# Half of an expert goes from the attention part into the seven-product part

## The chip, the cores and the metric

One core of a Trainium2 chip runs the whole program. The metric is the device time of one execution in microseconds (us). A core has five engines, each with its own instruction queue that is worked off in order: TensorE (PE in the profile; its weight loads are shown as PEld), VectorE (DVE), ScalarE (ACT), GpSimd (POOL) and SyncE (SP). They meet through semaphores. Transfers are issued by SP, ACT or POOL and carried by 16 DMA engines. Matrix products go to PSUM; VectorE and ScalarE copy ("evict") them to SBUF.

## The reference

```python
def _attn_ref(q_l, k_l, v_l, q_g, k_g, v_g):          # 8 batches, 8 heads, 512 local and 32 global tokens, head size 64
    k_all = np.concatenate([k_g, k_l], axis=2); v_all = np.concatenate([v_g, v_l], axis=2)
    out_g = np.matmul(sm(scale * np.matmul(q_g, k_all.transpose(0, 1, 3, 2))), v_all)
    s_ll = np.where(np.abs(pos[:, None] - pos[None, :]) <= 32, scale * np.matmul(q_l, k_l.transpose(0, 1, 3, 2)), -1e9)
    s_lg = scale * np.matmul(q_l, k_g.transpose(0, 1, 3, 2))
    out_l = np.matmul(sm(np.concatenate([s_lg, s_ll], axis=-1)), np.concatenate([v_g, v_l], axis=2))
    return np.concatenate([out_g, out_l], axis=2)

def _moe_ref(x, w_gate, w1, w2):                      # x: 4352 tokens of 512; 8 experts, 512 -> 1024 -> 512
    P = np.exp(logits - logits.max())                 # logits = x @ w_gate
    for _ in range(8):                                # rows and columns brought to equal sums, eight times
        P /= P.sum(1, keepdims=True) + 1e-09
        P /= P.sum(0, keepdims=True) + 1e-09
        P *= N / E
    for e in range(E):
        out += P[:, e:e + 1] * (np.maximum(x @ w1[e], 0.0) @ w2[e])
```

Every expert works on every token, so the eight experts' products are most of the work. N is 4608 in the source; the 4352 rows of this case are what the kernel computes.

## The kernel before, in words

**First part: attention in slots.** A loop over `s` from 0 to 33 treats one pair of heads of one batch in each slot (32 pairs, four slots to a batch, and two slots to drain). Its stages lie staggered: while slot `s` computes the scores of pair `s`, pair `s-1` gets its output and pair `s+1` is transposed.
- `st_A` transposes keys and queries on TensorE (L305). VectorE copies the keys from PSUM into the row `kTe` (L307), ScalarE the queries into `qbd` (L314, two copies).
- `st_B` computes scores in three groups of 3, 3 and 2 blocks of 64 queries. A block takes two products: 128 columns of local keys (L337) and 32 of global keys (L339). VectorE adds the mask and takes the maximum (L344), ScalarE the exponential (L347). The first group of slot `s` needs `qbd` of the copies at the end of slot `s-1`.
- `st_D1` transposes the weights (L354; VectorE copies them, L356), `st_D2` transposes the finished output of pair `s-2` and the weights of the global keys (L364, L368; ScalarE copies both, L370 and L372), `st_E` multiplies with the values (L388; VectorE divides, L392 and L393).
- The global queries' attention is in `st_G1` (even slots; ScalarE L412, VectorE L409) and `st_G2`, `st_G3`, `st_G3n` (odd slots; ScalarE L422 and L449).

Between these stages lie places for **pieces** of experts 0 and 1, which are computed plainly on the 512 tokens of a group `m` as soon as the group's attention is done: `p_l1` (four products of 512 columns, L475, evicted by ScalarE at L478 or VectorE at L480) and `p_l2` (eight products, L489, evicted at L492, stored to DRAM as `yd`). A slot has six places: four `p_l1` (evicted by ACT, ACT, DVE, DVE) and two `p_l2` (both ACT). In units of four products of 512 columns that is 8 units a slot. The order of all queues is the order in which Python emits the instructions; no scheduler changes it.

GpSimd issues the loads that convert to 16 bits. In slots 8 to 32 it also forms, for experts 2 to 7, sums and differences of weight quarters (`sums_load`, `sums_form`, 24 steps of four `tensor_tensor`, L120) and stores them to DRAM as `kept`. SP moves the values into their second layout (`load_v`, `move`) and loads the global values `vgz` and `vgn`.

**Between the parts**, eight rounds of row and column sums (`sk_rows`, `sk_cols`) run on VectorE with small products on TensorE; the remaining pieces (`tail`) fill TensorE.

**Second part: seven products for eight.** Experts 2 to 7 run in 12 stages, two passes of six: pass 0 on the first 2048 tokens, pass 1 on the other 2304. Both matrix products of an expert are split into two by two quarters and computed with seven quarter products and sums of quarters. A stage has 8 slots in pass 0 and 9 in pass 1; a slot is a `Slot` (first product, L908) interleaved with a `Unit` (second product, L810), each product group at a fixed place in `run_slot`. ScalarE copies partial results, VectorE forms token sums (L749), sums of hidden activations (L806), rectified sums (L912), and adds results into the output (L844). `fetch` loads a stage's weights (L726) and their sums from `kept` (L727, L728). `stored_add` (L765) adds the stored results of experts 0 and 1 during the stages. In the first four slots of the first stage the pieces still left in `tail` fill TensorE (`fill`).

Of the kernel before, what the change touches and what calls it, by code (L numbers as in the profile page):

```python
# [23 lines left out]
def kernel(  # L24
# [33 lines left out]
    VW = Dh + 1  # L58
    assert (B, H, Sl, Dh, Sg) == (8, 8, 512, 64, 32) and D == H * Dh and F % P == 0
# [33 lines left out]
    work = {}  # L93

# [33 lines left out]
    with ExitStack() as att:  # L128
# [8 lines left out]
        mask = att_c.tile([P, 3, SW], FP32)  # L137
# [3 lines left out]
        kTe = [att_c.tile([P, W + Sl + W], FP16, name=f"kTe{i}") for i in range(4)]  # L141
        vgr = [att_c.tile([P, 4 * H * VW], FP16, name=f"vgz{i}") for i in range(2)]
        vgz = [t.rearrange("p (a h v) -> p a h v", a=4, h=H) for t in vgr]
        vgn = [att_c.tile([P, H, VW], FP16, name=f"vgn{i}") for i in range(2)]
# [4 lines left out]
        vg16 = [dscr.tile([Sg, H, Dh], FP16, name=f"vg16_{b}") for b in range(B)]  # L149

# [8 lines left out]
        def load_vz(b):  # L159
            for i in range(4):  # L160
                nc.sync.dma_start(out=vgz[b % 2][i:P:4, i, :, 0:Dh], in_=vg16[b])
            nc.sync.dma_start(out=vgn[b % 2][P - Sg : P, :, 0:Dh], in_=vg16[b])

        def load_v(b):
# [11 lines left out]
            def last():  # L176
                nc.gpsimd.dma_start(out=vb[HB : HB + W, NJ - 1, :, 0:Dh], in_=src[Sl - W : Sl])
# [10 lines left out]
            def move():  # L188
                if b < 2:
                    return part  # L190
                nc.sync.dma_start(out=vb[96:P, NJ - 1], in_=va[W : 2 * W, 0])
                nc.sync.dma_start(out=vb[0:HB, :], in_=va[HB:P, :])
                nc.sync.dma_start(out=vb[HB:P, 0 : NJ - 1], in_=va[0:HB, 1:NJ])
                if b > 1:
                    load_vz(b)
# [66 lines left out]
        for t in (kTe[0], kTe[2], kTe[3]):  # L262
            nc.vector.memset(t[:, 0:W], 0.0)
            nc.vector.memset(t[:, W + Sl :], 0.0)
# [7 lines left out]
        def clear_z(i, eng):  # L272
            eng.memset(vgr[i].bitcast(mybir.dt.uint32), 0)
            eng.tensor_copy(out=vgz[i][:, :, :, Dh], in_=own.unsqueeze(2).to_broadcast([P, 4, H]))
            eng.memset(vgn[i][0 : P - Sg], 0.0)
            eng.memset(vgn[i][P - Sg : P, :, Dh:VW], 1.0)
# [15 lines left out]
        load_vz(0)  # L292

# [3 lines left out]
        def st_A(n):  # L297
# [4 lines left out]
            for t, src in enumerate((ks, qs)):  # L302
                for so in range(NJ):
                    for a in range(2):
                        nc.tensor.transpose(pt[t][HB * a : HB * (a + 1), P * so : P * (so + 1)],  # L305
                                            src[:, 2 * hp + a, so, :], identity)
            nc.vector.tensor_copy(out=kt[:, W : W + Sl].rearrange("c (p s) -> c p s", s=NJ),  # L307
                                  in_=pt[0].rearrange("c (s p) -> c p s", s=NJ))
            if n < NPL:
                nc.scalar.copy(out=qpl[n % 2].rearrange("c (p s) -> c p s", s=NJ), in_=pt[1].rearrange("c (s p) -> c p s", s=NJ))  # L310
                return
            for a in range(2):
# [4 lines left out]
        def st_B(n, part):  # L317
# [10 lines left out]
            for ii in range(ni):  # L328
                i = i0 + ii
                if n < NPL:  # L330
                    for c0, c1, kk in ((0, KW, kt[:, HB * i : HB * i + KW]), (KW, SW, kgT[:, hp, Sg * b : Sg * (b + 1)])):
                        for a in range(2):
# [3 lines left out]
                    continue  # L336
                nc.tensor.matmul(sc[:, SW * ii : SW * ii + KW], qb[:, i, :],  # L337
                                 kt[:, HB * i : HB * i + KW], start=True, stop=True)
                nc.tensor.matmul(sc[:, SW * ii + KW : SW * (ii + 1)], qb[:, i, :],  # L339
                                 kgT[:, hp, Sg * b : Sg * (b + 1)], start=True, stop=True)  # L340
            for ii in range(ni):
                i = i0 + ii
                mi = 0 if i == 0 else (2 if i == NHB - 1 else 1)
# [54 lines left out]
        def st_G1(b, g):  # L398
# [3 lines left out]
            for c0, c1, k0 in ((0, Sl - W, 2 * W), (Sl - W, Sl, W), (Sl, S, None)):  # L402
                for hh in range(4):
                    pr, a = divmod(hh, 2)
                    r = slice(HB * a, HB * (a + 1))
                    rhs = kgT[r, 2 * g + pr, gc] if k0 is None else kTe[(n0 + pr) % 4][r, k0 : k0 + c1 - c0]
# [18 lines left out]
        def st_G3(b, g):  # L425
# [3 lines left out]
            for t in range(5):  # L429
                for par in range(2):  # L430
                    r, h0 = slice(HB * par, HB * (par + 1)), 4 * g + 2 * par
                    rhs = vb[:, t, h0 : h0 + 2, :] if t < NJ else vgn[b % 2][:, h0 : h0 + 2, :]
# [75 lines left out]
        NU = B * HP  # L508
        nc.vector.tensor_copy(out=mask[:, 0, 0:KW], in_=mask[:, 1, 0:KW])
        nc.vector.tensor_copy(out=mask[:, 2, 0:KW], in_=mask[:, 1, 0:KW])  # L510
        nc.vector.memset(mask[:, 0, 0:W], NEG)
        nc.vector.memset(mask[:, 2, 3 * W : KW], NEG)
        st_A(0)
        unread(2, 256)
        first_keys()
        for s in range(NU + 2):
            b, hp = divmod(s, HP)
            if s < NU and b + 1 < B:
# [15 lines left out]
                if s == 5:  # L534
                    queue += [lambda: load_g(1, "kgs"), lambda: load_g(1, "qgs")]
# [554 lines left out]
```

## Time and profile before

| what | value |
|---|---|
| time, median of 3 runs (range) | 998.58 us (998.53 to 999.15) |
| the profiled execution's own time | 998.93 us |
| its span, first to last instruction | 997.2 us |
| granted TensorE clock, mean | 0.998 |
| TensorE busy | 982.5 us (99%), 8868 products |
| VectorE busy | 767.2 us (77%) |
| ScalarE busy | 655.5 us (66%) |
| GpSimd busy | 301.7 us (30%) |
| first product of the second part (L908) | at 356.26 us |

The span is what the prediction's sums are made against; 1.7 us of the execution's own time lie outside it, and the own time is 0.35 us above the median. A row of a timeline gives start, duration, engine, line, operation, output and inputs, count, and in brackets how long the engine had waited and for whom. A row of a table of stretches gives the stretch, its length, and then for each engine the busy time and the number of instructions, the granted clock, and the DMA share. Durations of products overlap their successors, so the cost of a product is read from start to start.

### The profile page before, as it was taken

The page shows a single profiled execution, that of the slowest core. Times are in us where ns is not written, and L with a number is a line of the kernel's source. Part 1 is how long each engine was busy: PE and PEld are TensorE (multiplying, and loading weights), DVE is VectorE, ACT ScalarE, POOL GpSimd, SP SyncE. Part 2 cuts the span into 40 slices and gives each one's busy share as a digit, 9 for nine tenths or more (in the row PEclk, how much of TensorE's full clock was granted, in tenths as well). Part 3 has the DMA queues.
Part 4 walks back from the last instruction along what each step waited for, and adds up shares of the span by engine and source line. Part 5 has one row for each costly group of instructions (what it writes and reads, how often), then busy time and mean ns, then how long its engine had stood idle before and what let it go on. Part 6 is the DMA issues. An engine that isn't in the chain of part 4 may idle for free.

```text
span 997.2 us, 22451 instructions
## 1 busy us (share of the span) xinstructions
PE 982.5 (99%) x8868; PEld 641.0 (64%) x8868; DVE 767.2 (77%) x1858; ACT 655.5 (66%) x1342; POOL 301.7 (30%) x364
## 2 busy tenths in 40 slices
PE   7899999999999999999999999999999999999998
PEld 4566566656665555666666666676767676776764
DVE  7866665666653755889999888997899999888885
ACT  6888888888884566765555555557765555555551
POOL 9748887888850102111111111111111111100000
PEclk9999999999999999999999999999999999999999
DMA  9999999999952387554543333575664543123043
GB/s 167 186 156 199 239 206 221 222 200 222 234 144 85 108 241 169 161 147 121 122 107 74 75 75 74 128 214 129 165 148 117 117 96 66 53 65 74 2 106 127
DMA packets 138058, 138.68 MB, mean 139 GB/s; under 512 B 56608, under 2 KB 110048, under 8 KB 135904
## 3 DMA queue, kind: packets, MB, share of 16 engines
q0 software_dynamic: 105696, 87.32, 49.6%
q1 hardware_dynamic: 31696, 49.60, 15.5%
q8 instruction: 69, 1.13, 0.5%
q10 hardware_dynamic: 560, 0.33, 0.1%
q14 instruction: 37, 0.30, 0.1%
HBM read 144.46 MB, written 39.58 MB: 185 GB/s over the span
## 4 chain that ended last, share of the span: by engine, by line
PE 94%; POOL 3%; DMA 1%; DVE 1%; issue 0%; SPq 0%; ACT 0%; POOLq 0%; DVEq 0%
PE z L810 30%; PE pa L908 18%; PE py L489 12%; PE ph L475 12%; PE pb L908 9%; PE pc L908 4%; PE po L388 1%; PE ptw L354 1%; PE zp L879 1%; PE sc L337 1%; DMA vgz<-vg 1%; PE pk L305 1%; PE tgx L364 1%; PE pq L305 1%; PE sg L407 0%; POOL va L174 0%
## 5 line engine op out<-in xcount | busy, mean ns | idle before, releaser
L810 PEld LDWEIGHTS <-hs 128*128 128x128 f16 x2264 | 220.7, 98 | 91.8 <-DVE hs L806 0.4
L810 PE MATMUL z<-w2e,hs 128*128 128x256 f16 x1304 | 195.6, 273 | 0.0
L810 PE MATMUL z<-v,hs 128*128 128x256 f16 x960 | 144.0, 273 | 0.0
L475 PE MATMUL ph<-xT,w1e 128*128 128x512 f16 (+1 forms) x576 | 129.3, 367 | 0.6 <-ACT xT L372 0.6
L347 ACT ACTIVATE Pu<-ms,mx 128x160 f16<-128x160 f32 x256 | 120.1, 636 | 13.3 <-DVE mx L344 10.4
L489 PE MATMUL py<-w2e,hT 128*128 128x512 f16 x544 | 128.2, 379 | 0.0
L831 ACT COPY z<-z 128x256 f32<-128x256 f32 x98 | 35.0, 357 | 141.7 <-PE z L810 141.7
L908 PEld LDWEIGHTS <-w1e 128*128 128x128 f16 x960 | 87.1, 98 | 51.6 <-issue 1.0
L908 PE MATMUL pa<-t,s 128*128 128x512 f16 x384 | 114.2, 379 | 0.0
L726 POOL DMA_DIRECT2D w1e<-in_moe_w_dram x24 | 17.5, 734 | 297.5 <-PE pa L908 220.4
L344 DVE CUSTOM_DVE_ANT_0 ms<-sc,mask 128x160 f32<-128x160 f32 x256 | 70.2, 320 | 46.6 <-ACT yst L492 30.0
L844 DVE SCALAR_TENSOR_TENSOR oy<-z,lg,oy 128x512 f32<-128x512 f32 x128 | 95.8, 749 | 7.6 <-ACT oy L849 5.1
L806 DVE TENSOR_TENSOR hs<-hs 128x512 f16<-128x512 f16 x224 | 94.9, 424 | 8.2
L912 DVE CUSTOM_DVE_ANT_0 hx<-pb,s 128x512 f16<-128x512 f32 x96 | 65.9, 687 | 36.4 <-ACT s L942 30.2
L726 POOL DMA_DIRECT2D w2e<-in_moe_w_dram x24 | 19.8, 833 | 243.6 <-PE z L810 214.2
L928 ACT ACTIVATE hs<-pa 128x512 f16<-128x512 f32 x96 | 57.2, 596 | 47.0 <-PE pa L908 46.9
L475 PEld LDWEIGHTS <-w1e 128*128 128x128 f16 x576 | 53.4, 98 | 52.9
L912 DVE CUSTOM_DVE_ANT_0 hs<-pb,s 128x512 f16<-128x512 f32 x96 | 65.9, 686 | 24.1 <-ACT s L942 23.7
L908 PEld LDWEIGHTS <-s 128*128 128x128 f16 x720 | 65.6, 98 | 28.5 <-issue 0.3
L489 PEld LDWEIGHTS <-hT 128*128 128x128 f16 x544 | 49.8, 98 | 51.9
L480 DVE TENSOR_SCALAR hT<-ph 128x512 f16<-128x512 f32 x58 | 40.1, 692 | 55.1 <-PE ph L475 55.0
L478 ACT ACTIVATE hT<-ph 128x512 f16<-128x512 f32 (+1 forms) x86 | 50.6, 588 | 28.8 <-PE ph L475 28.4
(197 smaller groups left out, 1971.0 us busy)
## 6 DMA issues: line engine op xcount, KB each, us to landing
ys<-yd SPq DMA_DIRECT2D x68, 256.0 KB, 3.2
yd<-yst SPq DMA_DIRECT2D x16, 1024.0 KB, 5.9
pw<-in_moe_w_dram POOLq DMA_DIRECT2D x24, 512.0 KB, 10.1
kept<-psum POOLq DMA_DIRECT2D x24, 512.0 KB, 5.3
s<-kept POOLq DMA_DIRECT2D x12, 768.0 KB, 8.9
v<-kept POOLq DMA_DIRECT2D x12, 768.0 KB, 8.9
w1e<-in_moe_w_dram POOLq DMA_DIRECT2D x12, 512.0 KB, 5.3
w2e<-in_moe_w_dram POOLq DMA_DIRECT2D x12, 512.0 KB, 6.7
```

Source lines behind the costliest of these rows:

```text
L344: nc.vector.tensor_tensor_reduce(out=ms[:, ii, :], in0=sc[:, SW * ii : SW * (ii + 1)], in1=mask[:, mi, :], scale=-scale, scalar=BIG, op0=A ...
L347: nc.scalar.activation(out=d["Pu"][:, i // 4, :, i % 4], in_=ms[:, ii, :], func=AF.Exp, scale=-1.0, bias=d["mx"][:, i : i + 1])
L475: nc.tensor.matmul(ph[:, 0:n], wts[e][0][:, dk, P * fm : P * (fm + 1)], xT[:, dk, c0 : c0 + n], start=(dk == 0), stop=(dk == DP - 1))
L478: nc.scalar.activation(out=hT[:, fm, 0:n], in_=ph[:, 0:n], func=AF.Relu)
L480: nc.vector.tensor_scalar(out=hT[:, fm, 0:n], in0=ph[:, 0:n], scalar1=0.0, scalar2=None, op0=ALU.max)
L489: nc.tensor.matmul(py, hT[:, fk, P * c : P * (c + 1)], wts[e][1][:, fk, :], start=(fk == 0), stop=(fk == FT - 1))
L806: nc.vector.tensor_tensor(out=o, in0=x, in1=y, op=op)
L810: nc.tensor.matmul(o, lhs[:, fk, :], rhs[:, fk, :], start=(first and fk == 0), stop=(fk == HF - 1), skip_group_check=True)
L844: nc.vector.scalar_tensor_tensor(out=o, in0=z, scalar=p, in1=o, op0=ALU.mult, op1=ALU.add)
L908: nc.tensor.matmul(o, lhs[:, dk, P * f : P * (f + 1)], rhs[:, dk], start=(first and n == 0 and dk == 0), stop=(dk == HD - 1), skip_group_c ...
L912: nc.vector._custom_dve(TENSOR_ADD_SAT, out=self.to(i, j), in0=self.of(ps), in1=self.of(s), s0=BIG, s1=0.0)
L928: nc.scalar.activation(out=self.to(1, 0), in_=self.of(self.pa), func=AF.Relu)
```

## The change

- Expert 1 is computed plainly only on groups 0 to 3. Its other 2304 tokens get a stage of their own in the second part, in pass 1 between experts 6 and 7 (13 stages).
- A slot of the first part has three places (`region`) in the stead of six. They take regions from one list of 84: two `p_l1` pieces, one `p_l2` piece, or (twice in nine) a single `p_l1`. Evictions alternate between ACT and DVE over the whole list.
- Rows of keys: from pair 6 on, a row has room for 24 times 32 keys. Each slot ScalarE copies the global keys into it (`k_global`, one more copy ahead of the two `qbd` copies), VectorE copies the local keys with three copies, and a block's scores are one product of 160 columns (for odd blocks of batch 1 still two). Odd blocks see their keys in another order, so the second layout of the values and one mask change too (five moves on SP in the stead of three, `load_vz` ahead of them, `vgn` single and loaded in the slot with `hp == 2`).
- GpSimd forms sums for experts 2 to 5 only (16 steps, in two slots of three, each formed two slots after its load). For experts 6 and 7 in pass 0 and for expert 1, VectorE forms them in the second part (`weight_sums`, 16 operations a stage, in place), and SP stores those of 6 and 7 for pass 1 (`keep`).
- `tail` ends with expert 1's group 3; the pieces that `fill` places are evicted by VectorE, and one `fill` place goes.

```diff
@@ helpers of the attention part
+    KC = 24
+    EARLY = range(2, 6)
+    sum_slots = [8 + n * 24 // 16 for n in range(4 * len(EARLY))]
...
+        def k_block(n, i):
+            kt, r = kTe[n % 4], i // 2 * 5 * W
+            if i % 2:
+                return kt[:, r + 4 * W : r + 9 * W]
+            return kt[:, r : r + 9 * W].rearrange("c (k w) -> c k w", w=W)[:, 0:9:2]
...
+        def k_global(n):
+            b, hp = divmod(n, HP)
+            kg = kTe[n % 4][:, 4 * W : 24 * W].rearrange("c (r k w) -> c r k w", k=5, w=W)[:, :, 4]
+            nc.scalar.copy(out=kg, in_=kgT[:, hp, Sg * b : Sg * (b + 1)].unsqueeze(1).to_broadcast([P, NJ, Sg]))
@@ move, in load_v
+                load_vz(b)
                 nc.sync.dma_start(out=vb[96:P, NJ - 1], in_=va[W : 2 * W, 0])
-                nc.sync.dma_start(out=vb[0:HB, :], in_=va[HB:P, :])
-                nc.sync.dma_start(out=vb[HB:P, 0 : NJ - 1], in_=va[0:HB, 1:NJ])
-                if b > 1:
-                    load_vz(b)
+                nc.sync.dma_start(out=vb[0:W, :], in_=va[HB : HB + W, :])
+                nc.sync.dma_start(out=vb[HB : HB + W, :], in_=va[HB + W : P, :])
+                nc.sync.dma_start(out=vb[W:HB, 0 : NJ - 1], in_=va[0:W, 1:NJ])
+                nc.sync.dma_start(out=vb[HB + W : P, 0 : NJ - 1], in_=va[W:HB, 1:NJ])
@@ st_A, from pair 6 on
+            for o in range(2):
+                ...
+                nc.vector.tensor_copy(out=kd, in_=ko[:, o])
+            nc.vector.tensor_copy(out=kt[:, 22 * W : 23 * W].rearrange("c (p s) -> c p s", s=NJ), in_=ko[:, 0, 0, 0])
+            k_global(n)
@@ st_B
-                nc.tensor.matmul(sc[:, SW * ii : SW * ii + KW], qb[:, i, :],
-                                 kt[:, HB * i : HB * i + KW], start=True, stop=True)
-                nc.tensor.matmul(sc[:, SW * ii + KW : SW * (ii + 1)], qb[:, i, :],
-                                 kgT[:, hp, Sg * b : Sg * (b + 1)], start=True, stop=True)
+                else:
+                    nc.tensor.matmul(sc[:, SW * ii : SW * (ii + 1)], qb[:, i, :], k_block(n, i), start=True, stop=True)
@@ the slots' places
+        seq = [(0, 0), (1, 0), (0, 1), (1, 1), (0, 2), (0, 3), (1, 2), (0, 4), (0, 5), (0, 6)]
+        regions = []
+        for g, (e, m) in enumerate(seq):
+            firsts = [[2 * i, 2 * i + 1] for i in range(FT // 2)]
+            if 0 < g < len(seq) - 1:
+                firsts[-1:] = [[FT - 2], [FT - 1]]
+            for i, fs in enumerate(firsts):
+                regions.append([lambda eng, e=e, m=m, f=f: p_l1(e, m, f, eng) for f in fs])
+                if g and (i < NJ - 1 or i == len(firsts) - 1):
+                    regions.append([lambda eng, c=min(i, NJ - 1), o=seq[g - 1]: p_l2(*o, c, eng)])
+        def region():
+            for f in regions.pop(0) if regions else ():
+                f("av"[evict[0] % 2])
+                evict[0] += 1
...
-            f1("a")
+            if s >= 6:
+                region()
             if s < NU:
                 st_B(s, 0)
...
-            f2("a")
+            if s >= 6:
+                region()
...
             if 7 <= s < NU:
                 st_B(s, 1)
-            f1("a")
...
-            f1("v")
+            if s >= 5:
+                region()
             if s < NU:
                 st_B(s, 2)
...
-            f2("a")
...
-            f1("v")
@@ tail and the second part
-        for e, m in ((0, B - 1), (0, B), (1, B - 1), (1, B)):
+        for e, m in ((0, B - 1), (0, B), (1, 3)):
...
-        stages = [(pas, e) for pas in range(2) for e in range(2, E)]
+        stages = [(0, e) for e in range(2, E)] + [(1, e) for e in (*range(2, E - 1), 1, E - 1)]
...
+        def here(k):
+            pas, e = stages[k]
+            return e == 1 or not pas and e not in EARLY
...
+            return [lambda o=o, x=x, y=y, op=op, r=r: nc.vector.tensor_tensor(out=o[:, r], in0=x[:, r], in1=y[:, r], op=op)
+                    for o, x, y, op in ops for r in parts]
...
             def fill(n):
                 for _ in range(min(n, len(tail)) if a is not None else 0):
-                    tail.pop(0)[1](pool=ps_z, tag="z")
+                    tail.pop(0)[1]("v", pool=ps_z, tag="z")
...
-            if x is None:
-                fill(1)
...
+                if here(k + 1):
+                    for i, at in enumerate((2, 3, 4, 5, 6, 6, 7, 7)):
+                        jobs[at].append(lambda i=i: weight_sums(k + 1, 0)[i]())
...
+            if here(k):
+                for i in range(8):
+                    jobs[i // 2].append(lambda i=i: weight_sums(k, 1)[i]())
+                jobs[0].append(lambda: keep(k, 0))
+                jobs[4].append(lambda: keep(k, 1))
```

## The prediction

> **What bounds the kernel.** I read the page first: busy times, then the chain of work that ended last.
>
> ```profile
> PE 982.5 (99%) x8868; PEld 641.0 (64%) x8868; DVE 767.2 (77%) x1858; ACT 655.5 (66%) x1342; POOL 301.7 (30%) x364
> PE 94%; POOL 3%; DMA 1%; DVE 1%; issue 0%; SPq 0%; ACT 0%; POOLq 0%; DVEq 0%
> ```
>
> TensorE is busy throughout and the chain is TensorE's own queue. So work taken from TensorE counts in full, until another engine sets the pace. To see how far off that is I read the table of stretches: columns are length, then busy time of PE, PEld, DVE, ACT, POOL.
>
> ```profile
> 25.00:50.00 25.00, 21.77 (x424) 14.80 (x423) 20.06 (x84) 21.99 (x51) 17.65 (x26) 1.00 1.55 186
> 163.84:245.10 81.26, 81.26 (x1026) 49.19 (x1025) 50.31 (x200) 68.90 (x146) 66.68 (x71) 1.00 1.16 212
> 459.50:508.10 48.60, 48.60 (x338) 32.85 (x337) 45.53 (x81) 27.65 (x57) 5.67 (x8) 1.00 0.50 119
> 557.20:599.80 42.60, 42.60 (x297) 28.80 (x296) 35.10 (x63) 24.28 (x51) 2.94 (x4) 1.00 0.33 76
> ```
>
> The second row is eight full slots: 10.16 us a slot, TensorE never idle, ScalarE busy 8.61, VectorE 6.29, GpSimd 8.33. The third and fourth are second-part stages, 6.08 us a slot: with stored results to add VectorE is busy 94%, without 82%. The first is slots before the pieces begin.
>
> Slot 7 of before has only four units and comes near to what a slot will hold afterwards. ScalarE's timeline of it, then TensorE's:
>
> ```profile
> 53.43 1.36 ACT L347 ACTIVATE Pu<-ms,mx 128x160 f16<-128x160 f32 x3
> 54.54 0.78 ACT L422 COPY pgs<-pt 128x640 f16<-128x640 f16 x1
> 55.23 0.36 ACT L370 COPY pg<-tgx 128x256 f16<-128x256 f16 x1
> 55.49 0.58 ACT L372 COPY xT<-tgx 128x512 f16<-128x512 f16 x1
> 55.97 1.37 ACT L347 ACTIVATE Pu<-ms,mx 128x160 f16<-128x160 f32 x3
> 57.08 0.68 ACT L478 ACTIVATE hT<-ph 128x512 f16<-128x512 f32 x1
> 58.01 1.01 ACT L347 ACTIVATE Pu<-ms,mx 128x160 f16<-128x160 f32 x2 [0.25 <-DVE mx L344]
> 58.77 1.28 ACT L314 COPY qbd<-pq 64x512 f16<-64x512 f16 x2
> ```
>
> ```profile
> 52.53 0.22 PE L337 MATMUL sc<-kTe,qbd 128*128 128x128 f16 x1
> 54.54 0.38 PE L364 MATMUL tgx<-identity,xn 128*128 128x128 f16 x4 [0.87 <-DVE pw L356]
> 60.19 0.22 PE L337 MATMUL sc<-kTe,qbd 128*128 128x128 f16 x1
> ```
>
> From first score to next first score this slot takes 7.66 us, though its TensorE work is 6.8. There is a ring: `qbd` (ends 60.05), score products (60.19), maxima, exponentials, the slot's ScalarE work in order, `qbd` again. Each slot must run through it; with 10.16 us of TensorE work it was hidden.
>
> **The change, part by part.** A unit is four products of 512 columns at 216 ns from start to start, 0.863 us.
>
> *Moved half expert.* Groups 4 to 7 (16 units each) and 8 (8 units) leave: 72 units, 62.2 us. The new stage has nine slots of 6.075: +54.7 us. Net -7.5, if TensorE stays the bound.
>
> *Score products.* The three groups of pairs take about 0.28, 0.25 and 0.25 us from their first start to the next product (56.84 to 57.09 is the last one of slot 7): 0.78 a slot. A product of 160 columns, between 128 (55 ns from start to start) and 256 (109), is some 69 ns: 0.55 a slot, -0.23.
>
> *TensorE's slot* is then 10.16 - 6.91 (8 units) - 0.23 + 4.60 (16 units in three slots) = 7.61 us. The single L1 regions make the slots uneven: 6, 6, 4 units.
>
> *ScalarE's slot.* Without its four evictions (0.65 twice, 0.53 twice) 8.61 becomes 6.25. It gets half of 12 evictions in three slots back, 1.24, and the global-key copy. That copy's nearest rows are 0.26 (256 columns, L370, start to start) and 0.31 (64 columns, L449); I take 0.25, with 0.15 and 0.40 as ends. Sum 7.74: as much as TensorE's 7.61. The Trainium skill, "VectorE: DVE Perf Modes", section "The TRN2 errata", gives a ScalarE copy of 128 elements within SBUF 350 cycles; at its 1.2 GHz that is an estimate of 0.29 us and would add 0.9 us to the whole. No row before shows the operation.
>
> *The ring.* Equal busy times on two engines that wait for each other do not both fit. From the rows: `qbd` to first score 0.14, first score to first exponential 0.90 (52.53 to 53.43), exponentials 1.11, 1.11 and 0.76, L422 or L412 with its wait 0.75, L370 and L372 0.74, global keys 0.25, `qbd` 1.28: 7.04 us. Evictions by ScalarE in the second and third place add 1.19 in the six-unit slots and 0.65 in the four-unit slot; one in the first place hides in the 0.90. So 8.23, 8.23, 7.69, mean 8.05. L449 ahead of a first-place eviction overfills the 0.90 in one slot of six (0.05), and VectorE's longer queue (three key copies of about 0.8 for 0.60, then L393, L446 and a first-place eviction) delays the masks by 0.3 in about two of six (0.1). I take 8.2. Lower end: 7.61, TensorE's own. Upper end: 8.8, ScalarE's 7.74 at the 88% that the first row above reaches in slots without pieces.
>
> *The first part.* From the first score of slot 8 (60.19) to that of slot 31 (293.89) are 23 slots, 233.7 us; at 8.2, 188.6: -45.1. Slots 6 and 7 get two units more each: +1.7, and +0.5 by the ring: +2.3. From there to the second part's first product (356.26) nine units go: -8.0 with the last scores. That product starts near 305.5.
>
> *Its start.* `fill` has 8 units for 14: -5.2. But the four tail products that stood between the stage's first products and waited out VectorE's token sums (357.67 to 362.8) are fewer. I count about 1 us in slot 0, 0.45 in the next three by ScalarE's copies, 1 where L912 queues behind 16 token sums: +3 (0.5 to 5).
>
> *Sums on VectorE.* 16 operations for each of three stages, 0.42 us, next start after 0.34 to 0.46. In the fourth stage (experts in order 2, 3, 4, 5) eight of them meet the 94% stretch: five slots 0.1 to 0.5 over, +1.2 (0 to 3.6, all eight exposed). In the stages of 6, 7 and 1 VectorE has 1.07 us a slot free, in which two fit. That pass 1 adds 18 stored results fewer saves nothing: TensorE bounds there.
>
> *Hidden.* GpSimd loses eight steps of 6.1 us; its slot, 2.2 for loads and two thirds of 6.1, is 6.3 of 8.2. SP has two moves more a batch, `vgz` ahead of them, and `vgn`, which waits for slot `hp == 1`'s last products; behind it stand the `yd` store and the moves. It lands 4.8 us after issue with 8 us to spare; without that cover it is 4.8 us a batch. The DMA share, 1.16 here and 1.55 in the first row, leaves room for a batch in 33 us with a third fewer sums. A late full-width weight load would hold VectorE: issued at 503.97 in the fourth stage, its first sum is due after slot 2, near 520; 512 KB took 5.3 to 10.1. Each later microsecond costs one.
>
> *Sum.* 2.3 - 45.1 - 8.0 - 5.2 + 3 + 54.7 + 1.2 = +2.9 us against the profiled execution's 998.93; that stands 0.35 above the median, so the median goes to 1001.5.
>
> **The rivals.**
> 1. *TensorE keeps the pace: faster.* For it: both sums are 7.6, the buffers are double, and before, no slot after 72 us shows a stall. Against it: slot 7. At 7.61 the 23 slots take 13.6 less: 988. The point from which it decides is a slot under 7.99; break-even is 8.07.
> 2. *No measurable change*, slots of 7.99 to 8.16: around 998.6. Within 0.2% (2 us) a measurement of this kernel, with a range of 0.6 us, hardly tells it from none.
> 3. *VectorE becomes the second part's bound.* The 94% stretch speaks for it, the 82% stretch against. With all eight sums exposed: 1004.
> 4. *The clock falls.* Short stops recur in each slot. The rows with idle TensorE, 21.77 of 25 us busy, were granted 1.00, which speaks against; at the 0.93 of the first 25 us TensorE's slot would be 7.61 / 0.93 = 8.18, still about the ring's, so 1002 to 1003. The Trainium skill, "TensorE: Matmul & The Clock Gate", section "A second HAM failure mode", says frequent micro-idles between product groups can make the gate oscillate between half and full clock. By that rule it would be much slower; the trace so far does not agree.
>
> **How the numbers follow.** Ring at 8.16 or more, with or without rival 3: 0.50, slower, 1001.5 the likeliest. Rival 1: 0.33, faster. Rival 2: 0.15. Rival 4: 0.02, slower. The ring at 8.8 gives 13.8 more; a start of 5 and sums of 3.6 could lift it further, but not all together. From rival 1's 988 to the ring's upper end I cut about one in ten on each side: 989 to 1009. The likeliest case alone has 999 to 1010.
>
> **What would show it.** First product of the second part near 305 us. Slots of 8.2, 8.3 and 7.7 us by first scores. TensorE 92 to 94% busy between 70 and 260 us, its idle time ended by ScalarE's `qbd` copies, ScalarE above 90% there. Score products 69 ns apart. VectorE at 98% or more in the fourth stage, and the new stage 54.7 us. The prediction is wrong if TensorE stays at 99% in the slots, or if waits for DMA or for VectorE's key copies stand where I have ScalarE's.

## The result and the profile after

The changed kernel takes 1004.97 us (median of six runs, 1004.26 to 1005.33) against 998.92 us for the kernel before (six runs): a ratio of 1.0055, 95% interval 1.0045 to 1.0065. It is 6 us slower. I had forecast 1001.5 us, slower, with 989 to 1009 as range. The profiled execution of the changed kernel has an own time of 1004.91 us and a span of 1003.1 us, 5.9 us more than before.

The page of the changed kernel, busy times and chain:

```profile
PE 980.0 (98%) x8744; PEld 644.0 (64%) x8744; DVE 822.6 (82%) x2028; ACT 654.7 (65%) x1369; POOL 245.6 (24%) x304
PE 86%; ACT 6%; DMA 3%; DVE 2%; POOL 2%; issue 1%; SPq 0%; DVEq 0%; POOLq 0%; ACTq 0%
```

TensorE's share of the chain falls from 94% to 86%, and ScalarE, at 0% before, has 6%. The table of stretches of the changed kernel shows where. The first row is the 23 slots from the first score of slot 8 to that of slot 31. The second is a stretch as long as a stage of the second part, most of it the fourth stage (452.70 to 501.40):

```profile
63.22:254.06 190.84, 182.64 (x2480) 110.80 (x2479) 147.79 (x620) 171.10 (x393) 135.92 (x147) 1.00 1.10 190
...
459.50:508.20 48.70, 48.70 (x338) 32.72 (x337) 47.00 (x89) 27.69 (x57) 1.64 (x2) 1.00 0.35 71
```

The slots take 8.30 us each instead of 10.16; TensorE is no longer without a gap, and ScalarE is busy 90%. In the second part TensorE still is without a gap, at 6.08 us a slot. TensorE's waits inside the 23 slots, from the view of waits (line waited for, by whom, us in total, times, longest):

```profile
PE sc L372 <- ACT qbd L345: 4.7, 11, 0.7
PE py L534 <- ACT hT L523: 2.9, 8, 0.6
PE tgx L396 <- DVE pw L388: 0.4, 1, 0.4
```

This view begins to count where the modelled end of the product before lies. Counted from start to start beyond the 0.216 us of a product, the same waits are 6.9 us for `qbd` (the rows of the first kind, two of them behind a `py`, and a few too short for the view), 4.2 us for the buffer of a `py`, 1.1 us for `pw` and 0.3 us at the logits: 12.5 us.

| stretch | forecast | measured (profiled runs) |
|---|---|---|
| start to first score of slot 8 | +2.3 | +3.0 (60.19 to 63.22) |
| 23 slots | -45.1 | -42.9 (233.70 to 190.84) |
| first score of slot 31 to the second part | -8.0 | -7.3 |
| first stage, its eight slots | -2.2 | -1.9 (48.24 to 46.32) |
| new stage | +54.7 | +54.8 |
| VectorE's weight sums | +1.2 | +0.1 |
| sum | +2.9 | +5.9 (the rest is rounding and 0.15 at the end) |

### The slots are not alike

The regions of three slots hold 6, 6 and 4 units. But the first region of a slot stands ahead of its first scores, so from first score to first score there are 6, 5 and 5 units. I call these windows A (a `py`, a pair, a `py`: slots 10, 13, ...), B (a pair, a `py`, a single: 8, 11, ...) and C (a single, a `py`, a pair: 9, 12, ...). Their means are 8.43, 8.62 and 7.86 us: the longest windows are B, which hold no more units than C. In A TensorE has next to no wait, in C one for `qbd` or for `pw`; in B it waits both for `qbd` and for the buffer of a `py`. Here is such a B, slot 20, of the changed kernel: rows of TensorE's timeline, then VectorE's, then ScalarE's (start, duration, engine, line, operation, tiles, count, in brackets the wait and its releaser).

```profile
163.18 0.37 PE L372 MATMUL sc<-kTe,qbd 128*128 128x160 f16 x3
...
167.11 1.89 PE L534 MATMUL py<-w2e,hT 128*128 128x512 f16 x8 [0.39 <-ACT hT L523]
...
170.15 1.04 PE L520 MATMUL ph<-xT,w1e 128*128 128x512 f16 x4
171.90 0.38 PE L372 MATMUL sc<-kTe,qbd 128*128 128x160 f16 x3 [0.71 <-ACT qbd L345]
```

```profile
163.38 0.69 DVE L539 COPY yst<-py 128x512 f32<-128x512 f32 x1 [0.23 <-PE py L534]
164.10 0.33 DVE L376 CUSTOM_DVE_ANT_0 ms<-sc,mask 128x160 f32<-128x160 f32 x1
```

```profile
164.47 1.37 ACT L379 ACTIVATE Pu<-ms,mx 128x160 f16<-128x160 f32 x3 [0.60 <-DVE mx L376]
165.86 0.71 ACT L457 ACTIVATE Pg<-sg,m 128x544 f16<-128x544 f32 x1
166.47 0.59 ACT L523 ACTIVATE hT<-ph 128x512 f16<-128x512 f32 x1
166.95 0.37 ACT L402 COPY pg<-tgx 128x256 f16<-128x256 f16 x1
167.20 0.61 ACT L404 COPY xT<-tgx 128x512 f16<-128x512 f16 x1
167.68 1.40 ACT L379 ACTIVATE Pu<-ms,mx 128x160 f16<-128x160 f32 x3
169.03 0.58 ACT L537 COPY yst<-py 128x512 f32<-128x512 f32 x1
169.64 1.01 ACT L379 ACTIVATE Pu<-ms,mx 128x160 f16<-128x160 f32 x2
170.41 0.36 ACT L170 COPY kTe<-kgT 128x128 f16<-128x128 f16 x1
170.67 1.17 ACT L345 COPY qbd<-pq 64x512 f16<-64x512 f16 x2
```

The reader is to see the ring of the prediction closed: scores at 163.18, masks, from 164.47 on ScalarE without a gap until `qbd` ends at 171.84, and scores at 171.90. It takes 8.72 us instead of the 8.23 that I had worked out, for the most part because VectorE evicts a `py` (163.38 to 164.10) before it can make the masks: the first exponential comes 1.29 us after the score, not 0.90. On the way an eviction by ScalarE (L523, 166.47) holds up a second place: the `py` at 167.11 needs the product buffer that it frees.

### The profile page after: what moved, and what is told of

Read it like the earlier page. It is cut to its first block, busy times and chain, and to the rows that moved or that the text cites. A ratio compares the mean times of both kernels' runs of the same rounds, so it can differ in the third digit from the quotient of the medians.

```text
span 1003.1 us, 22385 instructions
## 1 busy us (share of the span) xinstructions
PE 980.0 (98%) x8744; PEld 644.0 (64%) x8744; DVE 822.6 (82%) x2028; ACT 654.7 (65%) x1369; POOL 245.6 (24%) x304
## 4 chain that ended last, share of the span: by engine, by line
PE 86%; ACT 6%; DMA 3%; DVE 2%; POOL 2%; issue 1%; SPq 0%; DVEq 0%; POOLq 0%; ACTq 0%
PE z L889 33%; PE pa L987 19%; PE pb L987 10%; PE py L534 8%; PE ph L520 5%; PE pc L987 5%; ACT Pu L379 3%; PE zp L958 1%; PE sc L372 1%; ACT qbd L345 1%; DMA vgz<-vg 1%; PE ptw L386 1%; DMA vg<-in_v_g_dram 1%; PE po L420 1%; DMA yd<-yst 1%
## 5 line engine op out<-in xcount | busy, mean ns | idle before, releaser
L889 PEld LDWEIGHTS <-hs 128*128 128x128 f16 x2468 | 240.4, 98 | 100.1 <-DVE hs L885 1.0
L889 PE MATMUL z<-w2e,hs 128*128 128x256 f16 x1420 | 213.0, 273 | 0.0
L889 PE MATMUL z<-v,hs 128*128 128x256 f16 x1048 | 157.2, 273 | 0.0
L987 PEld LDWEIGHTS <-w1e 128*128 128x128 f16 x1056 | 95.4, 98 | 57.8 <-issue 3.1
L987 PE MATMUL pa<-t,s 128*128 128x512 f16 x416 | 123.8, 379 | 0.5 <-ACT s L1012 0.2
L534 PE MATMUL py<-w2e,hT 128*128 128x512 f16 x400 | 94.0, 379 | 2.9 <-ACT hT L523 2.9
L520 PE MATMUL ph<-xT,w1e 128*128 128x512 f16 (+1 forms) x416 | 95.4, 371 | 0.6 <-ACT xT L404 0.6
L987 PEld LDWEIGHTS <-s 128*128 128x128 f16 x792 | 71.9, 98 | 33.3 <-issue 2.5
L1021 ACT COPY s<-pa 128x512 f32<-128x512 f32 x111 | 64.9, 585 | 19.1 <-PE pa L987 6.7
L1012 ACT COPY s<-pa 128x512 f32<-128x512 f32 x111 | 65.0, 585 | 14.0 <-PE pa L987 2.8
L987 PE MATMUL pb<-xT,s 128*128 128x512 f16 (+1 forms) x264 | 66.1, 345 | 1.0 <-DVE hx L991 1.0
L987 PE MATMUL pc<-xT,w1e 128*128 128x512 f16 (+1 forms) x264 | 66.1, 345 | 0.1
```

The source lines that it names most:

```text
L520: nc.tensor.matmul(ph[:, 0:n], wts[e][0][:, dk, P * fm : P * (fm + 1)], xT[:, dk, c0 : c0 + n], start=(dk == 0), stop=(dk == DP - 1))
L534: nc.tensor.matmul(py, hT[:, fk, P * c : P * (c + 1)], wts[e][1][:, fk, :], start=(fk == 0), stop=(fk == FT - 1))
L889: nc.tensor.matmul(o, lhs[:, fk, :], rhs[:, fk, :], start=(first and fk == 0), stop=(fk == HF - 1), skip_group_check=True)
L987: nc.tensor.matmul(o, lhs[:, dk, P * f : P * (f + 1)], rhs[:, dk], start=(first and n == 0 and dk == 0), stop=(dk == HD - 1), skip_group_c ...
L1012: nc.scalar.copy(out=self.pre2, in_=self.pa)
L1021: nc.scalar.copy(out=self.pre3, in_=self.pa)
```

## The experiments

Times below are medians; each interval is that of the ratio to the kernel before, which ran beside them at 998.6 to 999.3 us. The changed kernel's is 1.0045 to 1.0065. The table after the last experiment has the windows of all of them.

### First round: which engine sets the slot

**Two products a block again, and no copy of the global keys** (one part undone):

```diff
-                    nc.tensor.matmul(sc[:, SW * ii : SW * (ii + 1)], qb[:, i, :], k_block(n, i), start=True, stop=True)
+                    kb = k_block(n, i)
+                    nc.tensor.matmul(sc[:, SW * ii : SW * ii + KW], qb[:, i, :],
+                                     kb[:, 0:KW] if i % 2 else kb[:, 0:4], start=True, stop=True)
+                    nc.tensor.matmul(sc[:, SW * ii + KW : SW * (ii + 1)], qb[:, i, :],
+                                     kgT[:, hp, Sg * b : Sg * (b + 1)], start=True, stop=True)
@@ st_A
-            k_global(n)
```

> One part undone: two score products a block as before (keys, then global keys from kgT), and no copy of the global keys by ScalarE. Ring through ScalarE (slot set by qbd, scores, masks, exponentials, qbd): the ring loses the 0.26 us copy, slots 8.05 to 8.1 instead of 8.30, 24 slots of them: about 999.5 us, although TensorE has 0.23 us more work in each slot. TensorE alone: +0.23 us a slot, about 1010.5. VectorE's queue: no change, 1005.

Measured: 1004.94 us (1.0032 to 1.0068), no change; the 23 slots take 190.29 us for 190.84. Two things cancel. From start to start TensorE's waits fall by 2.4 us, and its work grows by 1.9 us (0.08 us a slot, not the 0.23 that I had taken). The single score product with its key copy is worth nothing here either way. None of the theories had these two effects: the one of VectorE's queue names the time, but as the result of no effect at all.

**The next pair's `qbd` ahead of the last two blocks** (an order alone):

```diff
+            if s + 1 < NU and s >= 7:
+                st_A(s + 1)
             if s < NU:
                 st_B(s, 2)
...
-            if s + 1 < NU and s >= 7:
-                st_A(s + 1)
```

> Order alone: in the slots from 7 on the next pair's transposes, key copies and qbd come ahead of the scores, masks and exponentials of the last two blocks, so that these two exponentials (0.76 us) can fill the time between qbd and the next first exponentials (0.90). No operation added or removed. Ring: it is 0.76 us shorter and falls under TensorE's and ScalarE's own sums; slots 7.75 to 8.0, about 994 us (992 to 998). TensorE alone: no change, 1005. VectorE's queue: the three key copies now stand ahead of the last masks, no change or slower, 1005 to 1010.

Measured: 1010.79 us (1.0093 to 1.0131). A clear miss for my theory: 6 us slower, not 11 faster. The waits of TensorE in the slots of this kernel:

```profile
PE py L534 <- ACT hT L523: 3.4, 8, 0.5
PE pl L507 <- ACT qbd L345: 2.7, 4, 0.9
PE pl L507 <- DVE mx L376: 1.2, 2, 0.6
PE tgx L396 <- DVE pw L388: 1.0, 4, 0.3
```

The wait of the first scores for `qbd` is gone, as the ring says. But the logits' products (`pl`) now wait for a score buffer that `qbd` holds, and windows A, which had next to no waits, go from 8.43 to 9.07 us. The logits are not all of it: only two of the seven windows A have logits (slots 10 and 22, 9.71 us), and slots 13, 19 and 25, without, rise from 8.3 to 8.8 and 9.2 us too.

**More work for TensorE** (each first product of the output made twice):

```diff
                             i, h = 2 * j + par, 2 * hp + a
+                            if n >= 6 and first:
+                                nc.tensor.matmul(po[HB * par : HB * (par + 1), j, VW * a : VW * (a + 1)],
+                                                 d["pw"][:, i][:, HB * a : HB * (a + 1)], vab[b % 2][par][:, j, h, :],
+                                                 start=True, stop=True)
```

> 16 more products of 65 columns in each slot from 7 on (each first product of the output is made twice, about 18 ns each, 0.28 us a slot), behind the transposes of the next pair, where TensorE later waits for qbd. Ring: the wait takes them up, 1005 to 1006. TensorE alone: 26 times 0.28, about 1012.

Measured: 1009.63 us (1.0078 to 1.0115), between the two. The windows tell why: A grows by 0.34 us, B by 0.07, C by 0.10. The extra products themselves take 0.25 us a slot (759 ns for 505 from the first product of the output to the operation behind them). In five of the seven windows A TensorE is the bound and pays this in full, 0.25 to 0.29; slots 10 and 22 grow by 0.58, since a `py` there now waits 0.34 us for its buffer. In B and C TensorE's waits take most of the work up. So one pace for all slots, as the prediction had it, was the wrong picture.

**The global keys by GpSimd**:

```diff
-            nc.scalar.copy(out=kg, in_=kgT[:, hp, Sg * b : Sg * (b + 1)].unsqueeze(1).to_broadcast([P, NJ, Sg]))
+            nc.gpsimd.tensor_copy(out=kg, in_=kgT[:, hp, Sg * b : Sg * (b + 1)].unsqueeze(1).to_broadcast([P, NJ, Sg]))
@@ st_A
-            k_global(n)
+            if n < 8:
+                k_global(n)
@@ start of slot s
+            if s >= 7 and s + 1 < NU:
+                k_global(s + 1)
```

> The copy of the global keys is made by GpSimd at the start of the slot before, ahead of the sums in its queue; ScalarE's order is otherwise the same. Ring: 0.26 us a slot less, about 999 us (998 to 1001). TensorE alone: no change, 1005. If GpSimd's queue is what counts: the copy comes late behind the sums of the slot before, slower than 1005.

Measured: 1003.56 us (1.0017 to 1.0048). Taking 0.26 us from ScalarE in every slot gains 1.4 us, not 6: B loses 0.13 us, C 0.05, A 0.02.

### Second round: the places of the waits

**Evictions begun with VectorE:**

```diff
-                f("av"[evict[0] % 2])
+                f("va"[evict[0] % 2])
```

> Evictions of the pieces in slots: the same alternation between ScalarE and VectorE, begun with VectorE instead of ScalarE. No work added or removed. What the first four runs left: TensorE has no wait in slots of six units and two waits in those of five, before the first scores (for qbd, 6.2 us in 23 slots) and before a piece's py products (4.2 us, eight times 0.53, for ScalarE's eviction that frees the product buffer). If the py wait hangs on which engine evicts that one piece: it goes, about 1001 us. If ScalarE's and VectorE's queues are late as a whole: the wait turns up at another piece, 1005 (1003 to 1007).

Measured: 1003.65 us (1.0033 to 1.0063). The wait for the `py` buffer is gone but for 0.3 of its 4.2 us, and the one before the scores has grown from 6.9 to 9.8 us, both from start to start; one line is left in the view of waits:

```profile
PE sc L372 <- ACT qbd L345: 7.3, 11, 1.1
```

**`qbd` first, and the logits in the transposes' buffers:**

```diff
@@ beside the order of the second kernel above
-                logits(NJ * ((s - 6) // 4), NJ, ps_sc, "sc")
+                logits(NJ * ((s - 6) // 4), NJ, ps_tr, "tr")
```

> qbd ahead of the last two blocks as in e2, and the logits' products in the slots use the buffers of the transposes instead of those of the scores, where they waited for qbd (six waits of 0.63 to 1.01 in e2). If that wait is what cost e2 its gain: 1010.8 less 5 us, about 1005.5 (1004 to 1007), still no gain over the changed kernel since the other waits for evictions (py, pk) stay. If the three key copies ahead of the last masks cost it: 1010. If the ring was all that held TensorE: 998.

Measured: 1007.69 us (1.0069 to 1.0099), 3 us better than without the new buffers, and still slower than the changed kernel. Windows A stay at 8.90 us. The loss sits in the odd slots among them: 13, 19 and 25 take 0.9 to 1.2 us more than in the changed kernel, while 16 and 28 take 0.1 less. Slot 25 in TensorE's and ScalarE's timelines:

```profile
206.16 0.38 PE L372 MATMUL sc<-kTe,qbd 128*128 128x160 f16 x3
206.37 1.07 PE L386 MATMUL ptw<-identity,Pu 128*128 128x128 f16 x8
207.28 0.44 PE L465 MATMUL pt<-identity,Pg 128*128 128x128 f16 x5
```

```profile
204.93 1.17 ACT L345 COPY qbd<-pq 64x512 f16<-64x512 f16 x2
206.13 1.02 ACT L379 ACTIVATE Pu<-ms,mx 128x160 f16<-128x160 f32 x2
```

The last two exponentials now run behind `qbd`, until 207.15, and the weights' transposes `ptw`, which read them, stretch: the products behind them start 0.91 us after the first of them, against 0.45 in the changed kernel. Of this window's 9.21 us (8.27 in the changed kernel) that is half of the difference; the transposes of `Pg` behind take 0.54 for 0.28, most of the rest. In slots 16 and 28 these exponentials end before the scores begin (slot 16: at 130.92 us, scores at 131.04). So where ScalarE is late, what it does last in a slot is awaited at the start of the next, whichever of the two it is.

**One eviction in three by ScalarE:**

```diff
-                f("av"[evict[0] % 2])
+                f("avv"[evict[0] % 3])
```

> One piece in three is evicted by ScalarE, two by VectorE, instead of one in two each: ScalarE loses about 0.4 us a slot (two evictions of 12 in three slots), VectorE gets 0.45. If ScalarE's row of work is what TensorE waits for in the five-unit slots: 0.15 to 0.4 us in 16 of 24 slots, 999 to 1003. If VectorE's late masks count as much: no gain, 1004 to 1008. TensorE alone: 1005.

Measured: 1006.4 us (1.0054 to 1.0088), no gain. The 23 slots take 191.1 us for 190.84, with A at 8.33 (0.10 less) and B at 8.74 (0.12 more); what the whole is longer lies ahead of slot 8, whose first score is at 64.64 us for 63.22. Relief for ScalarE that lands on VectorE ahead of masks brings nothing.

**All six experts' sums by GpSimd again** (one part undone):

```diff
-    EARLY = range(2, 6)
-    sum_slots = [8 + n * 24 // 16 for n in range(4 * len(EARLY))]
+    EARLY = range(2, 8)
+    sum_slots = [8 + n for n in range(4 * len(EARLY))]
@@ each formed one slot after its load
-            if s - 2 in sum_slots:
-                sums_form(sum_slots.index(s - 2))
+            if s - 1 in sum_slots:
+                sums_form(sum_slots.index(s - 1))
```

> One part undone: GpSimd makes the sums of all six experts again, one step in each of 24 slots, and VectorE makes none for experts 6 and 7 in the second part. If VectorE's sums there are hidden: no gain in the second part. GpSimd's slot becomes 6.1 us of sums and 2.2 of loads, 8.3, as long as a slot. If that still hides: 1005. If loads of the next batch come late behind the sums: slots of 8.5 and more, 1010. If the sums on VectorE cost what I forecast: 1003.5.

Measured: 1010.84 us (1.0098 to 1.0128). The second part from its first product (L987 in these two kernels) to the end of the span takes 693.9 us, for 694.0 in the changed kernel (1003.1 - 309.13): VectorE's sums there cost 0.1 us at most. The loss is in one place, slot 25, which takes 14.80 us instead of 8.27:

```profile
PE po L420 <- DMA vb<-va: 4.0, 1, 4.0
```

```profile
SPq L182 <- DMA vg<-in_v_g_dram: 17.9, 1, 17.9
SPq L214 <- DMA va<-in_v_l_dram: 3.7, 1, 3.7
```

The first fence is TensorE's wait in that slot, the second what SP's queue waited for around it: values whose loads GpSimd issues. The wait, 4.2 us from start to start, is not the whole loss of 6.5. Behind it the granted clock (the number ahead of the last two) is half for the rest of the slot:

```profile
214.57:219.49 4.92, 4.92 (x49) 2.54 (x50) 1.52 (x5) 0.61 (x2) 4.44 (x4) 0.50 1.21 235
```

The eight `py` products there take 3.39 us (216.10 to 219.49) for 1.73 at full clock. All other slots are the same to 0.04 us. So the fewer sums of the change are worth about 6 us, as cover for the loads: 4.2 of waiting and some 2.3 of slower products behind it in the profiled execution. This kernel also forms its sums one slot after their load instead of two, so the size of that one delay is not the change's alone.

### Third round: evictions by place

**Who evicts is chosen by what the engine has to do at that place:**

```diff
-                regions.append([lambda eng, e=e, m=m, f=f: p_l1(e, m, f, eng) for f in fs])
+                regions.append([lambda e=e, m=m, f=f, one=len(fs) == 1: p_l1(e, m, f, "a" if f % 2 or one else "v") for f in fs])
...
-                    regions.append([lambda eng, c=min(i, NJ - 1), o=seq[g - 1]: p_l2(*o, c, eng)])
+                    regions.append([lambda c=min(i, NJ - 1), o=seq[g - 1]: p_l2(*o, c, "a" if c == 1 else "v")])
```

> The same pieces, the same evictions, six of twelve by each engine as in the changed kernel, but given out by place instead of in turn: in the first place of a slot ScalarE takes the piece that ends last (it has nothing to do between qbd and the first exponentials) and VectorE, which has the masks to make, only the earlier piece of a pair; of the later places ScalarE takes one piece a slot, never the one whose buffer the next py needs. Theory now: TensorE paces the slots of six units (8.3 to 8.6 us), a row of waits through VectorE's first masks and ScalarE the slots of five (8.24 on the mean in the changed kernel). If so, that row becomes 7.04 + 0.6 for one eviction + 0.1 to 0.3, 7.75 to 7.9 in 16 slots: 5.5 to 8 us less, 997 to 999.5. If the engines' sums decide: they have not changed, 1005.

**The same, and the global keys by GpSimd** (the edit shown above):

> As g1, and the copy of the global keys by GpSimd as in e4. If a row of waits through ScalarE sets the five-unit slots: 0.1 to 0.25 us less than g1 in 16 slots, down to what TensorE alone needs in them (7.5): 994.5 to 998, faster than both kernels. If the sums decide: 1003.5 as e4.

Measured: 1001.92 us (1.0017 to 1.0038) and 1000.17 us (1.0005 to 1.0023). The sums of the engines are those of the changed kernel and of the kernel with the copy on GpSimd, yet the first is 3.0 us and the second 4.8 us faster than the changed kernel. So the places count and not the sums; but the gain is half of what I expected. In the second kernel the view of waits has one place left:

```profile
PE sc L373 <- ACT qbd L346: 5.6, 9, 0.9
```

and in ScalarE's and VectorE's timelines of a window B one sees the next wait in line:

```profile
188.54 1.40 ACT L380 ACTIVATE Pu<-ms,mx 128x160 f16<-128x160 f32 x3
190.56 1.02 ACT L380 ACTIVATE Pu<-ms,mx 128x160 f16<-128x160 f32 x2 [0.62 <-DVE mx L377]
191.32 1.29 ACT L346 COPY qbd<-pq 64x512 f16<-64x512 f16 x2
```

```profile
189.59 0.69 DVE L540 COPY yst<-py 128x512 f32<-128x512 f32 x1 [0.80 <-PE py L535]
190.20 0.32 DVE L377 CUSTOM_DVE_ANT_0 ms<-sc,mask 128x160 f32<-128x160 f32 x1
```

ScalarE itself stands idle for 0.62 us, since VectorE evicts a `py` ahead of the last masks.

**Those evictions behind the masks:**

```diff
@@ p_l2: the eviction as a function, handed back where eng is "late"
-                    ... p_l2(*o, c, "a" if c == 1 else "v")])
+                    ... p_l2(*o, c, ("v", "a", "late", "late")[c])])
@@ slot
             if s < NU:
                 st_B(s, 2)
+            while late:
+                late.pop(0)()
```

> As g2, and VectorE evicts the third and fourth py of a group behind the masks of the slot's last two blocks instead of ahead of them. In g2 TensorE still waits 0.8 to 1.07 us for qbd in every second of the three kinds of slots, and ScalarE stands idle for 0.62 us in it, waiting for those masks behind that eviction (0.60). Theory: what holds TensorE is this row alone: last scores, masks, exponentials, qbd, next scores, where it has only one unit to do in between. Then the wait falls by 0.6 in 8 slots: 4.8 us, about 995.4 (994.5 to 997), faster than both kernels. If ScalarE's whole slot is the limit: its idle time moves to another place, 999 to 1000.5.

Measured: 1001.1 us (1.0014 to 1.0032), nothing gained. B falls from 8.31 to 8.04 as the theory has it, but C rises from 7.76 to 8.03 and A from 8.32 to 8.45: the eviction that was moved back pushes VectorE's copies and divisions into the next slot, and that slot's masks come late (in slot 24, a C, the first mask starts 1.02 us after the first score, for 0.52 without the move).

### Last: the link taken out

**No copies into `qbd` from pair 8 on:**

```diff
-            for a in range(2):
+            for a in range(2 if n < 8 else 0):
                 r = slice(HB * a, HB * (a + 1))
                 nc.scalar.copy(out=qb[r, :, HB * a : HB * (a + 1)].rearrange("c i (p s) -> c i p s", s=NJ),
```

> The changed kernel without the copies into qbd in the slots from the eighth pair on: all later pairs use the queries of the sixth and seventh, so this part of the computation is left out; TensorE's instructions stay the same, ScalarE loses 1.2 us a slot, and the first scores of a slot wait for nothing that ScalarE does. It measures TensorE's own slot. Theory: TensorE's own slot is 7.75 us on the mean (190.8 us of 23 slots, less some 12.5 of waits), so 23 slots take 178 and the kernel 992.5 us (991.5 to 995). If the slots of 8.3 are TensorE's own work: 1003 to 1005. If VectorE's masks and copies hold it as much as ScalarE: 997 to 1001.

Measured: 999.2 us, ratio 1.000 (0.9991 to 1.0009): the case "as much VectorE as ScalarE"; the theory, TensorE's own pace and 992.5 us, missed by 6.7. Its waits in the slots:

```profile
PE py L534 <- ACT hT L523: 2.7, 8, 0.6
PE tgx L396 <- DVE pw L388: 1.7, 4, 0.5
```

The 23 slots take 184.67 us. So the link through `qbd`, with the 1.2 us of ScalarE's work in it, is worth 6.2 us of the slots. From start to start another 6.6 us of waits for evictions and for `pw` are left, and without them TensorE's own work is 178 us, 7.74 us a slot. The same subtraction in the changed kernel (190.84 - 12.5) gives 7.75. No kernel here ran at that pace.

| kernel | time, us | 23 slots | A | B | C |
|---|---|---|---|---|---|
| changed | 1004.97 | 190.84 | 8.43 | 8.62 | 7.86 |
| pairs of products, no key copy | 1004.94 | 190.29 | 8.46 | 8.53 | 7.86 |
| `qbd` first | 1010.79 | 196.21 | 9.07 | 8.45 | 8.14 |
| more TensorE work | 1009.63 | 194.59 | 8.77 | 8.69 | 7.96 |
| key copy by GpSimd | 1003.56 | 189.23 | 8.40 | 8.49 | 7.81 |
| evictions begun with VectorE | 1003.65 | 189.85 | 8.49 | 8.49 | 7.81 |
| `qbd` first, logits elsewhere | 1007.69 | 193.56 | 8.90 | 8.43 | 7.98 |
| one eviction in three by ScalarE | 1006.4 | 191.10 | 8.33 | 8.74 | 7.85 |
| 24 sums by GpSimd | 1010.84 | 197.43 | 9.36 | 8.63 | 7.86 |
| evictions by place | 1001.92 | 188.36 | 8.33 | 8.45 | 7.80 |
| by place, key copy by GpSimd | 1000.17 | 186.80 | 8.32 | 8.31 | 7.76 |
| the same, late evictions | 1001.1 | 187.69 | 8.45 | 8.04 | 8.03 |
| no `qbd` copies | 999.2 | 184.67 | 8.32 | 8.01 | 7.80 |

The 23 slots and windows are from one profiled execution each. No kernel beats the one before; the best complete one, by place with the copy on GpSimd, comes within 1.4 us of it.

## Why the prediction was right, and where its steps were not

**The verdict and its reason held.** The forecast was that TensorE's waits in the slots eat what the moved work saves, and they do: TensorE's own work is 178.3 us in the 23 slots, and 12.5 us of waits come on top. Without these waits the slot would be 7.75 us, below the break-even of 8.07 that rival 1 needed; with them it is 8.30. Rivals 1 and 2 are out.

**The slot of 8.2 us was the right size by two errors.** First, *TensorE's slot* of 7.61 is 7.75. The term that was mis-sized is the score products. I priced eight of them at 69 ns, and at 69 ns (80 at most) they do follow each other. But the 0.78 us that I took this from was read up to the next product, and so holds what a change of tile shape adds behind a group: 0.08 us (107 ns from the last 32-column product to transposes in 64 columns, for 26 where the shape stays). The 0.55 has nothing for it, though it is still there: 0.09 us in the changed kernel (162 ns for 69), behind three groups in two slots. So the three groups take 0.21 or 0.22, 0.21 and 0.23 us, and 0.30 to 0.31 for the first where the global queries follow, against 0.25, 0.25 and 0.25, and 0.33. That saves 0.08 us, not 0.23, and the kernel with pairs of products shows the same 0.08. Second, *the ring* I summed as 8.23, 8.23 and 7.69 for slots of 6, 6 and 4 units. Between first scores there are 6, 5 and 5 units, TensorE alone paces the A windows (8.32 of 8.43), and the ring runs in B and C, where it takes 8.24 on the mean for the 8.05 of the sum: the delay of the masks by VectorE's longer queue, which I had at 0.3 in about two of six, is 0.39 in the window shown, and it comes back wherever work is put ahead of masks. That 8.2 came within 0.1 us of the measured 8.30 was in part luck: it is a mean over slots of 6, 6 and 4 units that the windows do not have, with a ring in the one third where TensorE sets the pace.

**The ring is not one engine's.** I read it as ScalarE's row of work with `qbd` as its link. Taking the link out gives 6.2 us of the slots, half of the waits; the other half are product buffers that wait for evictions and `pw` that waits for VectorE. Moving a piece of the row to another engine or to another place gave anything from 6 us lost to 4.8 gained, where I had expected 4 to 11 gained: each time another wait took its place. What sets B is which of the two engines is late at that place, and of this the sum had only the 0.1 for VectorE's queue.

**ScalarE's slot** I put at 7.74; the row gives 171.10 / 23 = 7.44, and the key copy is a part of that: where GpSimd makes it, ScalarE's busy time in the 23 slots falls from 171.10 to 167.54, by 0.16 a slot and not 0.25. The rest of the 0.30 stays open. The share I named as the sign, above 90%, is 89.7%. *TensorE 92 to 94% busy* reads 95.7%, and 93.4% if the waits are counted from start to start.

**The global-key copy** was well taken: 262 ns from start to start for 0.25 forecast. The Trainium skill, "VectorE: DVE Perf Modes", section "The TRN2 errata", by its cycle count gives the estimate of 0.29 us that the prediction named; this trace has 0.26 between starts and 0.36 to 0.40 for the instruction by itself.

**VectorE's sums** I put at +1.2 us in the fourth stage. The stage takes 48.70 us for the 48.63 of those before it, with VectorE busy 96.5% in the stretch shown with the result, not 98%, and the kernel that takes the sums of experts 6 and 7 away again has a second part of the same length within 0.1 us. They fit. Rival 3 is out.

**The rest.** The second part begins at 309.13 us, not near 305: the start is 0.7 us longer than forecast, the slots 2.2 and the stretch behind them 0.7, which is where the forecast of the whole falls short. The new stage was right to 0.1 us (54.8), the first stage to 0.3, and GpSimd's and SP's steps are hidden: no wait of TensorE in the slots is ended by a transfer. That cover is thin, as the kernel with 24 sums shows.

**Rival 4, the clock.** The granted clock is 1.00 in the slots although TensorE stops for 0.2 to 0.9 us at a time in two windows of three. The Trainium skill, "TensorE: Matmul & The Clock Gate", section "A second HAM failure mode", lets the clock swing under frequent short stops between groups of products; this trace does not agree. A single longer stop did lower it: in the kernel with 24 sums the clock was 0.50 behind the wait of 4.2 us.

**What stays open.** Whether some order of the evictions reaches TensorE's 7.75 us a slot. By the sums (7.44 for ScalarE, 6.43 for VectorE) it is not excluded; none of the orders tried came there, and 23 slots at that pace would take the changed kernel to about 992.5 us (1004.97 - 12.5), which is worked out and not shown.

## What to carry to other kernels

When work is taken from an engine that was never idle, its new time is not its own sum: look for the rows of work that other engines must finish once per iteration, and add them up window by window, from the same event to the same event, since places ahead of that event belong to the window before. Where two helpers are each busy 75 to 90% and hand work to each other, an order that removes one wait shows the next one, and it pays first to ask for each place which helper has something urgent behind the piece that it is given. A saving that only shortens one engine's list is worth what the window's last wait lets through: 0.26 us off ScalarE in every slot was worth 0.07 on the mean.

## What the runs showed of the hardware that I had not expected

- A group of products costs more at its end than between its members where the next operation has another tile shape: 160-column products follow each other after 69 to 80 ns, and products or transposes of the same shape start 69 ns after the last one, but transposes in 64 columns 162 ns after it. Behind a product of 32 columns it is 107 ns for 26. The change adds 0.08 to 0.09 us either way.
- The 16 extra products of 65 columns lengthen the stretch of products that they join by 0.25 us, 16 ns each: in the trace they start in pairs, the two 3 to 4 ns apart and the pairs about 31 ns.
- TensorE's stops of 0.2 to 0.9 us left the granted clock at 1.00 over 190 us; behind one stop of 4.2 us it was 0.50 for the next 4.9 us and more.
- VectorE busy 96.5% over a stretch as long as a stage, with TensorE waiting for it at other places of the same kernel, cost TensorE at most 0.1 us in 48.6.
